# Maxima of v and of the first weight group taken across partitions on GpSimd instead of TensorE, with new durations in the planner

## The chip, the cores and the metric

One core of one Trainium2 chip. The metric is the device time of one execution in microseconds (us), as the median of several runs. The engines are named as in the profile: PE is TensorE (PEld its weight loads), DVE VectorE, ACT ScalarE, POOL GpSimd, SP SyncE, which issues the DMAs.

## The reference, cut to what matters

```
# q, k, v: 4 x 12 x 448 x 64
scores = q @ k^T / 8 - log(448)
x = sigmoid(scores) @ v                      # heads joined: 4 x 448 x 768
u = x + real(fft(fft(x, axis=1), axis=2))
un = (u - mean(u)) / sqrt(var(u) + 1e-6)     # over the 768 columns
x2 = u + relu(un @ w_ch1) @ w_ch2            # 768 -> 3072 -> 768
gate = sigmoid(causal conv of x2 over 5 rows)
out = (gate * (x2 @ w_val)) @ w_out
```

## The kernel before, in words

All large products but those of the attention run on operands that are split into two f16 parts, a high and a low one. A split needs a power of two that scales the tensor, and so the largest absolute value of all its elements. The elements lie over 128 partitions; each engine finds the maximum along a partition, and then the 128 maxima have to be joined. The kernel has two ways for that. `peak` (L405) multiplies the identity `eye` by the column of maxima on DVE (the tile `pd`), lets PE multiply it by a matrix of ones (`ones_r`), so that each partition gets all 128 numbers in PSUM, and reduces them on DVE. `peak_pool` (L421) gives the column to GpSimd's `partition_all_reduce`. From the joined maximum five to six tiny DVE operations (`pow2`, `scaled`) make the scales: for v of one batch `ve`, `vi`, `st`, `rt`; for a weight matrix `w1e`, `w1i`, `w1s` (or `w2...`).

The work has four batches of 448 rows and passes through these stages, which overlap. (1) 84 score steps: each makes a block of 8 matmul rows `ps_s<-q,k` (QK below, with the step's number), a sigmoid `sg` on ACT, and a block `ps_m<-sg,v` (SV); DVE adds and ACT copies finished sums into `acc`. (2) For each finished batch the Fourier mixing: folds `pm` on DVE and POOL, halves `ph`/`pl` scaled by `st`, two rounds of matmuls (`cd,ph`, then `cs,zh`). (3) A layer norm: a mean matmul `tt,ones` over column sums `tt`, squares `tt<-tt` on ACT, DVE and POOL, a variance matmul `ones,tt`, `rs` by a power on POOL, four diagonal tiles `tt<-eye,rs` on DVE, and a matmul `tt,ones` over them ("rstd" below) that spreads the result, from which `un` is made. (4) An MLP in 8 groups of 384 hidden columns (`w1`, `w2`). (5) The gated output. Weights arrive as int64 and are converted on ACT and DVE (`wabs`, `wf`). The first group is made during stages 1 to 3, the other seven during the MLP.

The order on the engines is fixed when the kernel is built. `Board` holds jobs (Python generators); each yields the engine and the tiles it needs next. Between two PE steps `pump` emits what by the planner's clock (`Clock.note`, a table of durations for each kind of operation) can start without delay. Every engine then runs its operations strictly in the order in which they were emitted. So a duration in the table changes no instruction by itself, but it can change which job comes next, on all engines and queues. `peak_pool` adds a rule of its own: what uses its result is emitted when the planner's PE time has passed the reduce by 4.0 us. Since every operation is issued through the recording helper `call` of `Timed`, all of them bear its line, L212.

Of the kernel before, what the change touches and what calls it, by code (L numbers as in the profile page):

```python
# [43 lines left out]
COLS = 384  # L44
# [16 lines left out]
class Clock:  # L61
# [90 lines left out]
    def note(self, e, op, a, k):  # L152
        if op == "matmul":
            out, w, x = a
            n = x.free_size()
            full = x.partition_size() > 64 or w.free_size() > 64
            passes = 1 if x.dtype != F32 else 4 if full else 1
            cost = passes * (max(n / 2384, 0.045) + 0.004)
            mode = full, out.partition_size() > 64 or not full
            if mode != self.mode:  # L160
                cost += 0.2
                self.mode = mode
            return self.put("PE", cost, (w, x), (out,), 0.12, tag="mm")
        if op == "dma_start":
            out, src = k["out"], k["in_"]
            start = max(self.at["SP"], self.ready("SP", src), self.free("SP", out))
            self.at["SP"] = start + 0.4
            size = out.partition_size() * out.free_size() * mybir.dt.size(out.dtype)
            self.dma = max(self.dma, start + 1.4) + size / 215e3
            done = self.dma + 0.6  # L170
            self.log.append(("SP", None, start, start, done))
            return self.touch("SP", (src,), (out,), done)
        k = dict(k)
        if op in ("memset", "tensor_copy", "reciprocal"):
            for nm, x in zip(("out", "in_"), a):
                k.setdefault(nm, x)
        if op == "partition_all_reduce":
            k = dict(out=a[0], in_=a[1])
        out = k["out"]
        reads = [v for nm, v in k.items() if nm not in ("out", "accum_out") and hasattr(v, "tensor")]  # L180
        ins = [k[nm] for nm in ("in0", "in1", "in_") if nm in k and hasattr(k[nm], "tensor")]
        writes = [out] + ([k["accum_out"]] if k.get("accum_out") is not None else [])
        n = max([out.free_size()] + [x.free_size() for x in ins])
        sb = all(x.space != PSUM for x in ins)
        shared = False
        if e == "ACT":
            cost = 0.16 + n * 0.00095 + (0.19 if len(writes) > 1 else 0)
        elif e == "POOL":
            cost = 1.03 if k.get("op") == ALU.pow else 0.41 if op == "partition_all_reduce" else 0.12 + n * (0.002 if out.dtype == F16 else 0.00224)
            shared = op == "tensor_tensor"  # L190
        elif op in ("tensor_tensor", "scalar_tensor_tensor"):
            cost = 0.147 + n / 960
            shared = sb
        elif op in ("tensor_scalar", "tensor_copy") and sb and len(writes) == 1:
            cost = 0.16 + n / 1920
            shared = n > 4
        else:
            cost = 0.147 + n / 960 + (0.083 if len(writes) > 1 else 0)
        return self.put(e, cost, reads, writes, shared=shared, tag=op)
# [40 lines left out]
def on(e, *aps, cost=0.6, go=None):  # L240
    return (e,) if isinstance(e, str) else e, aps, cost, go


def when(go):
    return (), (), 0, go
# [89 lines left out]
def body(tc, qd, kd, vd, w1d, w2d, cwd, wvd, wod, cdd, k12d, csd, eyed, out):  # L335
# [30 lines left out]
    def ps_m():  # L366
        board.force(closed)
        tag = min(closed(), key=lambda g: ck.next_free(("ps", g), 1))
        p = ps.tile([128, 512], F32, tag=tag, bufs=1, name="ps_m")
        taken[tag] = p  # L370
        return p

    def done_m(p):
        for tag, q in list(taken.items()):
            if q is p:
                del taken[tag]

    def banks(n):
        return lambda: sum(board.by(ck.next_free(("ps", g), 1) - 0.1) for g in closed()) >= n
# [16 lines left out]
    def col(nm):  # L396
        return keep.tile([128, 1], F32, tag=nm, bufs=4 if nm in ("st", "rt", "x2e") else 2, name=nm)
# [4 lines left out]
    def peak(m, nm):  # L402
        yield on("DVE", m, eye)
        t = col(nm + "t")
        V.tensor_reduce(out=t, in_=m, axis=AX.X, op=ALU.max)  # L405
        d = keep.tile([128, 128], F32R, tag="pd", bufs=2, name="pd")
        V.tensor_scalar(out=d, in0=eye, scalar1=t, scalar2=None, op0=ALU.mult)
        yield on("PE", d, go=banks(1))
        p = ps_m()
        T.matmul(p[:, :128], ones_r, d, start=True, stop=True)  # L410
        yield on("DVE", p[:, :128])
        g = col(nm + "g")
        V.tensor_reduce(out=g, in_=p[:, :128], axis=AX.X, op=ALU.max)
        done_m(p)
        return g

    def peak_pool(m, nm):
        yield on("DVE", m)
        t = col(nm + "t")
        V.tensor_reduce(out=t, in_=m, axis=AX.X, op=ALU.max)  # L420
        yield on("POOL", t)  # L421
        g = col(nm + "g")
        P.partition_all_reduce(g, t, 128, ABSMAX)
        then = ck.at["POOL"] + 4.0
        yield when(lambda: board.by(then))
        return g

    def pow2(g, nm, upper=False):

        e = col(nm + "e")  # L430
        if upper:
            V.tensor_scalar(out=e.bitcast(I32), in0=g.bitcast(I32), scalar1=0x07F00000, scalar2=3, op0=ALU.bitwise_and, op1=ALU.logical_shift_left)
            V.scalar_tensor_tensor(out=e.bitcast(I32), in0=g.bitcast(I32), scalar=0x40000000, in1=e.bitcast(I32), op0=ALU.bitwise_and, op1=ALU.bitwise_or)
        else:
            V.tensor_scalar(out=e.bitcast(I32), in0=g.bitcast(I32), scalar1=0x7F800000, scalar2=None, op0=ALU.bitwise_and)
        V.tensor_scalar(out=e, in0=e, scalar1=2.0 ** -90, scalar2=2.0 ** 90, op0=ALU.max, op1=ALU.min)
        i = col(nm + "i")
        V.reciprocal(out=i, in_=e)
        return e, i
# [51 lines left out]
    def split_weight(pl, scratch, src, res, shape, exp, nm, bufs=1, early=False):  # L491

        n = shape[1] * shape[2]
        t = wp.tile([128, n], F32, tag="wf", bufs=1, name="wf")
        m = keep.tile([128, 18], F32, tag="wm", bufs=2, name="wm")
        yield from to_f32(scratch, src, t, n, m, W_RANK if early else 4)
        g = yield from (peak if early else peak_pool)(m[:, :n // COLS], nm)
        yield on("DVE", g)
        e, i = pow2(g, nm, True)
        s = scaled(i, 2.0 ** exp, nm + "s")  # L500
        yield when(lambda: not isinstance(pl, Later) or pl.at is not None)
        hi = pl.tile(shape, F16, tag=nm + "hi", bufs=bufs, name=nm + "hi")
        lo = pl.tile(shape, F16, tag=nm + "lo", bufs=bufs, name=nm + "lo")
        res += [hi, lo, e]
        h, l = (x.rearrange("p a b -> p (a b)") for x in (hi, lo))
        for c in range(0, n, n // 4):
            cc = slice(c, c + n // 4)
            if early:
                yield on("ACT", t[:, cc], s, cost=0.76)
                A.activation(out=h[:, cc], in_=t[:, cc], func=AF.Copy, scale=s)  # L510
                yield on("DVE", h[:, cc])
                V.scalar_tensor_tensor(out=l[:, cc], in0=t[:, cc], scalar=s, in1=h[:, cc], op0=ALU.mult, op1=ALU.subtract)
            else:
                yield on("ACT", t[:, cc], s, cost=0.76)
                A.activation(out=t[:, cc], in_=t[:, cc], func=AF.Copy, scale=s)
                yield on("ACT", t[:, cc], cost=0.68)
                A.activation(out=h[:, cc], in_=t[:, cc], func=AF.Copy)
                yield on("POOL", h[:, cc])
                P.tensor_tensor(out=l[:, cc], in0=t[:, cc], in1=h[:, cc], op=ALU.subtract)
# [95 lines left out]
    def scale_v(b):  # L615
        m = keep.tile([128, NT], F32, tag="vm", bufs=2, name="vm")
        for j in range(NT):
            i = b * NT + j
            yield when(lambda: i in vraw)
            x = vraw[i][:, :4 - j % 2]  # L620
            yield on("DVE", x)
            amax(x, m, j)
            maxed.add(i)
        g = yield from peak(m, "v")
        yield on("DVE", g)
        e, i = pow2(g, "v")
        st = scaled(i, 2.0 ** X_EXP, "st")
        rt = scaled(e, 2.0 ** -X_EXP, "rt")
        st_of[b] = st, rt
# [520 lines left out]
    for part, n in blocks:  # L1150
        g, b = n // B, n % B
# [167 lines left out]
```

## Time and profile before

| | |
|---|---|
| median of 3 runs | 1036.89 us (1036.79 to 1037.39) |
| the profiled execution: its time, its span | 1034.22 us, 1032.4 us |
| busy: PE, DVE, ACT, POOL | 1017.3, 699.3, 427.2, 175.4 us |

The span runs from the first to the last instruction that the profiler saw in one execution; 1.8 us of that execution's time lie outside it. The rows further below are of this execution, in us from the start of its span.

### The profile page before, as it was taken

How to read it: one execution, taken by the hardware profiler on the slowest of the kernel's cores; microseconds unless marked ns; L12 is line 12 of the kernel's file. 1: busy time of each engine (PE TensorE's matmuls, PEld its weight loads, DVE VectorE, ACT ScalarE, POOL GpSimd, SP SyncE). 2: the span in 40 equal slices, each digit the busy share in tenths (PEclk: the TensorE clock that was granted, in tenths of full speed). 3: DMA queues.
4: the chain of work that ended last, by engine and by line, in shares of the span. 5: the costliest groups of instructions: out<-in, count | busy, mean ns of one | idle time of the engine just before them, and what ended most of it. 6: DMA issues, size and time to landing. Idle time of an engine off the chain costs nothing.

```text
span 1032.4 us, 15544 instructions
## 1 busy us (share of the span) xinstructions
PE 1017.3 (99%) x6116; PEld 530.8 (51%) x6116; DVE 699.3 (68%) x1486; ACT 427.2 (41%) x633; POOL 175.4 (17%) x152
## 2 busy tenths in 40 slices
PE   9999999989999999999999999999999999999998
PEld 4354455665554555555555555555555455555554
DVE  4858888988567766666776657666777876775530
ACT  6776766333332234333233331333323745333321
POOL 0104412132201212220221220222202530000000
PEclk9999999999999999999999999999999999999999
DMA  7652230011233322223322312232331000000001
GB/s 230 200 187 92 86 124 2 3 35 43 62 92 93 92 62 78 61 77 92 92 77 62 85 53 75 66 91 52 87 93 48 1 1 1 10 36 37 37 30 69
DMA packets 33033, 72.57 MB, mean 70 GB/s; under 512 B 3860, under 2 KB 15552, under 8 KB 32960
## 3 DMA queue, kind: packets, MB, share of 16 engines
q1 hardware_dynamic: 32960, 71.58, 23.9%
q8 instruction: 48, 0.79, 0.3%
q14 instruction: 25, 0.20, 0.1%
HBM read 65.88 MB, written 5.51 MB: 69 GB/s over the span
## 4 chain that ended last, share of the span: by engine, by line
PE 89%; DVE 6%; ACT 2%; POOL 1%; issue 1%; DMA 0%; ACTq 0%; SPq 0%; DVEq 0%
PE ps_m L212 56%; PE ps_s L212 33%; DVE wf L212 1%; DVE acc L212 1%; DVE gp L212 1%; DVE pm L212 1%; ACT wf L212 1%; DVE wabs L212 0%; POOL w1lo L212 0%; POOL un L212 0%; DVE tt L212 0%; DMA w<-w2d 0%; POOL w2lo L212 0%; ACT w2hi L212 0%; ACT w1hi L212 0%
## 5 line engine op out<-in xcount | busy, mean ns | idle before, releaser
L212 PE MATMUL ps_s<-un,w1hi 128*128 128x448 f16 x1152 | 312.0, 352 | 0.0
L212 PE MATMUL ps_m<-hh,w2lo 128*128 128x448 f16 x576 | 203.0, 352 | 0.5 <-POOL w2lo L212 0.5
L212 PE MATMUL ps_m<-hh,w2hi 128*128 128x448 f16 x576 | 203.0, 352 | 0.0
L212 PE MATMUL ps_s<-un,w1lo 128*128 128x448 f16 x576 | 203.0, 352 | 0.0
L212 PE MATMUL ps_m<-hl,w2hi 128*128 128x448 f16 x576 | 203.0, 352 | 0.0
L212 DVE SCALAR_TENSOR_TENSOR acc<-ps_m,rg,acc 128x448 f32<-128x448 f32 x192 | 130.8, 682 | 59.7 <-PE ps_m L212 57.6
L212 PEld LDWEIGHTS <-w2hi 128*128 128x128 f16 x1152 | 112.6, 98 | 104.6 <-issue 0.5
L212 PEld LDWEIGHTS <-w1hi 128*128 128x128 f16 x1152 | 112.3, 98 | 105.0 <-issue 1.2
L212 DVE SCALAR_TENSOR_TENSOR wf<-w,wf 128x384 int32<-128x384 int32 x240 | 135.2, 563 | 5.7
L212 DVE SCALAR_TENSOR_TENSOR hl<-ps_s,hh 128x896 f16<-128x896 f32 x64 | 54.9, 857 | 116.9 <-ACT hh L212 116.6
L212 ACT ACTIVATE wabs<-w 128x384 f32<-128x384 f32 x112 | 60.8, 554 | 165.5 <-DMA w<-w1d 48.1
L212 ACT ACTIVATE sg<-ps_s,logb 128x896 f32<-128x896 f32 x84 | 83.6, 1006 | 33.4 <-PE ps_s L212 32.5
L212 ACT ACTIVATE hh<-ps_s 128x896 f16<-128x896 f32 x64 | 46.4, 725 | 106.5 <-PE ps_s L212 106.5
L212 PE MATMUL ps_m<-sg,v 64*64 64x448 f32 x672 | 83.4, 542 | 1.1 <-DVE acc L212 1.1
L212 PEld LDWEIGHTS <-w2lo 128*128 128x128 f16 x576 | 56.4, 98 | 53.8 <-POOL w2lo L212 1.3
L212 PEld LDWEIGHTS <-w1lo 128*128 128x128 f16 x576 | 56.4, 98 | 52.6
L212 PE MATMUL ps_s<-q,k 64*64 64x448 f32 x672 | 82.7, 538 | 0.5 <-ACT sg L212 0.5
L212 DVE SCALAR_TENSOR_TENSOR gp<-acc,cw,gp 128x448 f32<-128x448 f32 x84 | 62.0, 740 | 25.7 <-ACT gp L212 23.7
L212 PE MATMUL ps_m<-xs,wvhi 128*128 128x448 f16 x288 | 78.0, 352 | 0.0
L212 DVE TENSOR_SCALAR_CACHE_REDUCE wabs<-wabs 128x384 f32<-128x384 f32 x120 | 65.4, 545 | 2.2 <-ACT wabs L212 2.1
L212 DVE TENSOR_SCALAR wf<-wabs 128x384 int32<-128x384 int32 x120 | 43.2, 360 | 13.1 <-POOL w1lo L212 7.8
L212 PE MATMUL ps_m<-xs,wvlo 128*128 128x448 f16 x144 | 50.8, 352 | 0.0
(155 smaller groups left out, 1145.0 us busy)
## 6 DMA issues: line engine op xcount, KB each, us to landing
w<-w1d SPq DMA_DIRECT2D x48, 384.0 KB
w<-w2d SPq DMA_DIRECT2D x48, 384.0 KB
q<-qd SPq DMA_DIRECT2D x24, 224.0 KB
out<-o SPq DMA_DIRECT2D x24, 224.0 KB
k<-kd SPq DMA_DIRECT2D x23, 224.0 KB
w<-wvd SPq DMA_DIRECT2D x12, 384.0 KB
w<-wod SPq DMA_DIRECT2D x12, 384.0 KB
v<-vd SPq DMA_DIRECT2D x12, 256.0 KB
```

The costliest lines, as they stand in the source:

```text
L212: return f(*a, **k)
```

## The change

Two calls of `peak` become calls of `peak_pool`: the one for v (once for each of the four batches) and the one for the first weight group (once for `w1`, once for `w2`). The four calls of `peak` for `x2` late in the kernel stay. The planner's durations change in the second and third decimal: a one-pass matmul of 448 columns counts 0.1885 instead of 0.1919 us, a float32 one 0.006 instead of 0.004 us above its columns, an ACT operation some 1% less, and operations with more than 4 columns that read a scale from a tile 0.06 us more.

```
-            cost = passes * (max(n / 2384, 0.045) + 0.004)
+            cost = passes * (max(n / 2400, 0.045) + (0.0018 if passes == 1 else 0.006))
...
+        extra = 0.06 if any(hasattr(k.get(nm), "tensor") for nm in ("scalar", "scalar1", "scale")) and n > 4 else 0.0
         if e == "ACT":
-            cost = 0.16 + n * 0.00095 + (0.19 if len(writes) > 1 else 0)
+            cost = 0.155 + n * 0.00094 + (0.19 if len(writes) > 1 else 0) + extra * (n < 600)
...
-            cost = 0.147 + n / 960
+            cost = 0.147 + n / 960 + extra
...
-            cost = 0.16 + n / 1920
+            cost = 0.16 + n / 1920 + extra
...
-        g = yield from (peak if early else peak_pool)(m[:, :n // COLS], nm)
+        g = yield from peak_pool(m[:, :n // COLS], nm)
...
-        g = yield from peak(m, "v")
+        g = yield from peak_pool(m, "v")
```

In the built program six matmuls `ps_m<-pd,ones_r` are gone from PE (5399 to 5393 matmuls), six `pd<-eye` and six reduces of PSUM from DVE, and six reduces have come to POOL. The order is another on every engine.

POOL's order before, from the first memsets of the program (row 6 there) up to the variance of batch 0; `ISA` is an instruction without a tile, `acc_96`, `acc_98`, `acc_100` and `acc_102` are `acc` of batches 0 to 3:

```order
L212 MEMSET acc_102 128x6x4
L212 ISA
L212 TENSOR_TENSOR pm<-acc_96 128x448 x3
L212 TENSOR_TENSOR pm<-acc_98 128x448 x3
L212 TENSOR_TENSOR tt<-acc_96 128x448
L212 TENSOR_TENSOR tt<-tt,acc_96 128x448
L212 TENSOR_TENSOR pm<-acc_98 128x448
L212 TENSOR_TENSOR tt<-tt,acc_96 128x448 x3
L212 TENSOR_TENSOR tt<-tt 128x448 x4
L212 TENSOR_TENSOR rs<-rs,half 112x4
L212 TENSOR_TENSOR pm<-acc_100 128x448
```

The same stretch of POOL's order now, in the changed kernel:

```order
L213 ISA
L213 TENSOR_TENSOR pm<-acc_96 128x448
L213 ISA
L213 ISA vg<-vt 128x1
L213 ISA w1g<-w1t 128x1
L213 ISA
L213 TENSOR_TENSOR pm<-acc_96 128x448 x2
L213 TENSOR_TENSOR pm<-acc_98 128x448
L213 ISA
L213 ISA vg<-vt 128x1
L213 ISA
L213 TENSOR_TENSOR pm<-acc_98 128x448 x4
```

Each visit to the reduce now stands between two bare ISA rows: v of batch 0 and `w1` share the first visit, v of batch 1 has the second.

POOL's order now at the two later visits of the early part, v of batch 2 and then v of batch 3 with `w2`; the first row is from the norm of batch 0:

```order
L213 TENSOR_TENSOR tt<-tt 128x448 x3
L213 ISA
L213 ISA vg<-vt 128x1
L213 ISA
L213 TENSOR_TENSOR rs<-rs,half 112x4
...
L213 TENSOR_TENSOR tt<-tt 128x448 x2
L213 ISA
L213 ISA vg<-vt 128x1
L213 ISA w2g<-w2t 128x1
L213 ISA
L213 TENSOR_TENSOR pm<-acc_102 128x448
L213 TENSOR_TENSOR rs<-rs,half 112x4
```

The third visit stands between the squares and the power of the norm of batch 0, the fourth between those of batch 1.

DVE's order before, from the maxima of v of batch 0 and of `w1` on:

```order
L212 TENSOR_REDUCE vt<-vm 128x1
L212 TENSOR_SCALAR pd<-eye,vt 128x128
L212 SCALAR_TENSOR_TENSOR wf<-w_316,wf 128x384 x2
L212 TENSOR_REDUCE w1t<-wm 128x1
L212 TENSOR_SCALAR pd<-eye,w1t 128x128
L212 TENSOR_REDUCE vg<-ps_m 128x1
L212 TENSOR_SCALAR ve<-vg 128x1
...
L212 TENSOR_SCALAR rt<-ve 128x1
L212 TENSOR_REDUCE w1g<-ps_m 128x1
L212 TENSOR_TENSOR acc_96<-acc_96,ps_m 128x448
```

The same place in DVE's order now:

```order
L213 TENSOR_REDUCE w1t<-wm 128x1
L213 TENSOR_TENSOR acc_96<-acc_96,ps_m 128x448
L213 TENSOR_TENSOR pm<-acc_96 128x448
L213 TENSOR_SCALAR ve<-vg 128x1
...
L213 TENSOR_SCALAR rt<-ve 128x1
L213 TENSOR_REDUCE vm<-v 128x1
L213 TENSOR_SCALAR w1e<-w1g 128x1
...
L213 TENSOR_SCALAR w1s<-w1i 128x1
L213 TENSOR_TENSOR acc_96<-acc_96,ps_m 128x448
L213 TENSOR_TENSOR pm<-acc_96 128x448
```

The sum into `acc_96` moved ahead of the scales; the scales, and behind them the next sum into `acc_96`, now stand behind a result of POOL.

## Rows read from the trace of the kernel before

**Rows 1.** The page, busy time and share of the span

```profile
PE 1017.3 (99%) x6116; PEld 530.8 (51%) x6116; DVE 699.3 (68%) x1486; ACT 427.2 (41%) x633; POOL 175.4 (17%) x152
```

**Rows 2.** Waits of PE by releaser: total us, times, longest us

```profile
PE ps_m L212 <- DVE pd L212: 4.3, 4, 1.6
```

**Rows 3.** Timeline of PE at the first two pd: start, us, operation [idle before <-releaser]

```profile
32.88 0.94 PE L212 MATMUL ps_s<-q,k 64*64 64x448 f32 x8
34.98 0.33 PE L212 MATMUL ps_m<-pd,ones_r 128*128 128x128 f32 x1 [1.16 <-DVE pd L212]
36.43 0.33 PE L212 MATMUL ps_m<-pd,ones_r 128*128 128x128 f32 x1 [1.12 <-DVE pd L212]
...
37.49 0.93 PE L212 MATMUL ps_s<-q,k 64*64 64x448 f32 x8
...
43.51 0.93 PE L212 MATMUL ps_s<-q,k 64*64 64x448 f32 x8
```

**Rows 4.** Timeline of PE: norms of batches 0 and 2, a lone pd

```profile
95.57 1.02 PE L212 MATMUL ps_m<-tt,ones 128*128 128x448 f32 x2 [0.85 <-POOL tt L212]
...
106.79 0.93 PE L212 MATMUL ps_s<-q,k 64*64 64x448 f32 x8
...
108.71 0.93 PE L212 MATMUL ps_s<-q,k 64*64 64x448 f32 x8
...
116.62 1.15 PE L212 MATMUL ps_m<-tt,ones 112*128 112x112 f32 x8
...
119.36 1.20 PE L212 MATMUL ps_m<-cd,ph 128*113 128x385 f16 x6
...
122.80 1.07 PE L212 MATMUL ps_m<-sg,v 64*64 64x448 f32 x6
...
210.95 1.15 PE L212 MATMUL ps_m<-tt,ones 112*128 112x112 f32 x8 [2.15 <-DVE tt L212]
```

**Rows 5.** Timeline of PE, the first of four pd of x2

```profile
815.94 0.33 PE L212 MATMUL ps_m<-pd,ones_r 128*128 128x128 f32 x1 [1.56 <-DVE pd L212]
```

**Rows 6.** Timeline of POOL at the first reduce that the kernel before makes there

```profile
268.52 0.41 POOL L212 PARTITION_ALL_REDUCE w1g<-w1t  x1 [15.92 <-DVE w1t L212]
276.80 4.99 POOL L212 TENSOR_TENSOR w1lo<-wf,w1hi 128x576 f16<-128x576 f32 x4 [7.87 <-ACT w1hi L212]
```

**Rows 7.** Waits of POOL by releaser: total us, times, longest us

```profile
POOL w2lo L212 <- issue: 38.1, 5, 8.0
```

**Rows 8.** Timelines of DVE and ACT behind the reduce at 268.52

```profile
269.47 0.14 DVE L212 TENSOR_SCALAR w1e<-w1g 128x1 int32<-128x1 int32 x1
...
270.42 0.78 ACT L212 ACTIVATE wf<-wf,w1s 128x576 f32<-128x576 f32 x1 [8.30 <-DVE w1s L212]
```

**Rows 9.** Timelines of POOL, DVE and ACT in the score stage

```profile
30.10 1.58 POOL L212 TENSOR_TENSOR pm<-acc 128x448 f32<-128x448 f32 x1 [29.11 <-DVE acc L212]
...
43.80 1.58 POOL L212 TENSOR_TENSOR pm<-acc 128x448 f32<-128x448 f32 x1 [4.18 <-DVE acc L212]
...
102.42 2.35 POOL L212 TENSOR_TENSOR tt<-tt 128x448 f32<-128x448 f32 x2 [1.49 <-ACT tt L212]
...
110.80 1.31 POOL L212 TENSOR_TENSOR rs<-rs,half 112x4 f32<-112x4 f32 x1 [1.83 <-DVE rs L212]
...
115.05 0.28 DVE L212 TENSOR_SCALAR tt<-eye,rs 112x112 f32<-112x112 f32 x1
...
40.97 0.78 ACT L212 ACTIVATE w1hi<-wf,w1s 128x576 f16<-128x576 f32 x1
41.65 0.99 ACT L212 ACTIVATE sg<-ps_s,logb 128x896 f32<-128x896 f32 x1
```

**Rows 10.** Timeline of PE at the start of the span

```profile
1.03 4.19 PE L212 MATMUL ps_m<-ones 128*128 128x128 f32 x18 [1.03 <-DVE logb L212]
```

**Rows 11.** Windows: length, busy PE, PEld, DVE, ACT, POOL, granted clock, DMA share, GB/s

```profile
1028.50:1032.00 3.50, 0.17 (x1) 0.00 (x0) 0.00 (x0) 0.63 (x1) 0.00 (x0) 1.00 0.17 66
1032.00:1036.00 4.00, 0.00 (x0) 0.00 (x0) 0.00 (x0) 0.00 (x0) 0.00 (x0) 0.75 0.00 0
```

## The prediction

> **What bounds the kernel now.** I read the busy times first: PE works 1017.3 of 1032.4 us [rows 1], so the whole kernel holds about 15 us in which PE stands still, and no change that leaves the matmuls alone can gain more than that. The second view is PE's waits by releaser: the largest is the tile `pd`, 4.3 us in four waits [rows 2]. That is what `peak` costs directly. The third view is PE's timeline at these places, because a wait is only part of the price (the matmul and the change of tile shape come on top). In the score stage PE alternates QK and SV blocks; eight of them take 43.51 - 37.49 = 6.02, so 0.7525 us each [rows 3]. From QK19 at 32.88 to QK20 at 37.49 are two blocks, 1.51 us, and the two pd of v and `w1`; these cost 4.61 - 1.51 = **3.1 us** [rows 3]. A pd whose maxima are there in time costs 108.71 - 106.79 - 1.51 = **0.4 us** [rows 4]; two more in the score stage are like it. The fourth reading is PE's later waits: 2.15 us on `tt` before the rstd matmul of batch 2 [rows 4], and 1.56 us on the first pd of x2 [rows 5].
>
> **What a visit to the reduce costs.** The later groups show it, where GpSimd has time. The reduce takes 0.41 us at 268.52, but POOL's next operation starts at 276.80, 7.87 us after its end [rows 6]. That this is no wait for data shows in POOL's waits: before `w2lo` it stood five times for 38.1 us in all, 7.6 each, and waited for nothing that the profile shows [rows 7]. The bare ISA row behind each reduce in the order sits exactly there: something is loaded back. I take **7.7 us** behind each visit. The result itself is out early: DVE starts `w1e` at 269.47, 0.95 us after the reduce's start, and ACT uses `w1s` 0.95 later, at 270.42 [rows 8].
>
> Ahead of each reduce stands the same ISA row, but its time can't be read: POOL was idle for 15.92 us there until DVE had the column [rows 6], so a load could hide in it. Its bounds are 0 and 15.9. I take 7.7 too, by the nearest row, the same instruction behind the reduce. The planner counts 0.41 us for the whole visit, so it places other POOL work around it as if POOL were free.
>
> The Trainium skill (GPSIMD Engine Reference, 2.1 Instruction dispatch) says that the first call to freshly loaded GpSimd code pays a load of about 6 us that no instruction in the profile shows; the gaps here are longer, 7.6 to 7.9 [rows 6, 7]. With its 6 us ahead of each reduce the sum below would be about +3 instead of +10.
>
> **The change part by part.** Four visits come into the early part. Times are those of before, until the place in question.
>
> A, v of batch 0 and `w1`. POOL ends its first fold at 30.10 + 1.58 = 31.68 [rows 9]. With the load, `vg` runs to 31.7 + 7.7 + 0.4 = 39.8 and `w1g` from there; ACT can use `w1s` 0.95 + 0.95 later, at 41.7. In ACT's order `w1hi` stands ahead of the sigmoid of QK22, as before; it takes 0.7 (40.97 to 41.65), the sigmoid 1.0 [rows 9], so QK24, which needs the bank that this sigmoid frees, starts at about 43.8. Before it started at 43.51, with the 3.1 us of both pd in it [rows 3]. So the pd are gone and the wait for the sigmoid takes their place: +0.3. POOL's other two folds come after the load back, at 40.2 + 7.7 = 47.9 and later; the last of them began at 43.80 before [rows 9]. It is some 5 us late, the halves `ph` are late after it, and ACT's in-order queue holds a sigmoid behind `ph`: an estimate of +0.4 (0 to 1). A together **+0.7**. If the load were nothing, A would be -3.1, and it stays there up to a load of 4 us, since the column of `w1` is ready only shortly before its pd at 36.43 [rows 3].
>
> B, v of batch 1. POOL has only folds around it, which have slack; the lone pd goes: **-0.2** (-0.4 to 0).
>
> C, v of batch 2, is the dear one, since it stands between the squares and the power of batch 0's norm. The mean matmul is at 95.57 [rows 4]; POOL's third square ends at 102.42 + 2.35 = 104.77 [rows 9], 9.2 behind it. Then load 7.7, reduce 0.4, load back 7.7, power 1.3 [rows 9], four diagonals of 0.28 [rows 9]: 27.4 behind the mean. PE's rstd matmul has its place 116.62 - 95.57 = 21.0 behind the mean, less 0.4 for the pd that stood between, 20.6 [rows 4]; the order now has as many blocks there. So PE waits 27.4 - 20.6 = 6.8; less the pd itself, 0.4: **+6.4** (without the first load -0.4).
>
> D, v of batch 3 with `w2`, the same in batch 1's norm, with two squares on POOL instead of three: they end some 8.3 behind the mean (estimate: 9.2 less most of a square). Then 7.7 + 0.4 + 0.4 + 7.7, a fold 1.4 that stands ahead of the power, power 1.3, diagonals 1.1: 28.3. PE's place for rstd is there 20 blocks (15.1 us), two Fourier steps of 122.80 - 119.36 = 3.4 [rows 4] and about 1 us each for mean and variance matmul behind the mean's start: 23.9. So 4.4 late, first part of it at the variance matmul, since the scales of v on DVE hold squares behind them; and a sum into `acc` that is queued on DVE behind the diagonals keeps a PSUM bank from PE for some 1.5 more. Removed: a pd, 0.4, and the wait of 2.15 on `tt` at 210.95, since batch 2's norm now falls elsewhere. **+3.3**.
>
> x2. Its four pd stay, but the order has ten matmuls instead of five between the maxima and the first pd, so of the 1.56 us [rows 5] about 1.0 goes: **-1.0**.
>
> The clock. The first nine matmuls of 128 columns take 4.19 us [rows 10], where one of 448 columns in the score stage takes 1.02 [rows 4], so the nine would take some 2.2 there: PE begins at the lower of its two levels, 1.2 GHz, and loses 2.0 us. At the end, with PE idle from 1028.7 on (0.17 us busy in the window from 1028.5), the granted clock of the window from 1032 on has fallen to 0.75 on the mean [rows 11]. Whether it falls in the wait at C too, and costs 2.0 afterwards, is open: **+1.0** (0 to 2).
>
> The planner's durations, otherwise: a reshuffle with no visible place of its own; 0 (-1.5 to +1.5, as the waits of about 1 us of before would go or come). DVE loses six diagonals and six reduces of 0.28 us, but does not bound.
>
> Sum: 0.7 - 0.2 + 6.4 + 3.3 - 1.0 + 1.0 = **+10.2 us**. On the profiled execution this is 1034.2 to 1044.4; its time lies 2.7 below the median of the runs shown, and the difference applied to the median gives 1036.9 + 10.2 = **1047**.
>
> **The rivals.** (1) The load ahead of the reduce is short or is done ahead of time. For it: no row shows it. Against it: the same instruction behind the reduce shows 7.7. With nothing there, A is -3.1, B -0.4, C -0.4 (the diagonals come at 19.7, before PE's place at 20.6), D -2.5, x2 -1.0: -7.4, so **about 1030**, faster. It decides at a load of about 5 us: at 5, A -2.1, C +3.7, D +0.2 to -0.9, B and x2 -1.2, sum about 0. Below that every us saves about 1 at C and at first at D; above it A, C and D each pay.
> (2) A load ahead of about 6 us: A -1.0, B -0.2, C +4.7, D +0.7, x2 -1.0, the clock perhaps +0.3: **about 1040**, slower all the same. The rule of the skill's page above would end here.
> (3) The load ahead takes most of the 15.9 us bound: A, C and D each pay 7 us more, **about 1070**.
> (4) PE's clock falls at C and again at D, or DVE's order behind `ve<-vg` starves PE of banks for longer than I count: **1050 to 1054**.
> (5) The planner's durations do more than the visits, to either side; bounded above by the 15 us of idle time, but no place for it is seen.
>
> **How the numbers follow.** My forecast, a load of 6.5 to 9 ahead and 7.7 behind: 0.50 (1042 to 1051). Rival 2 or a load a little shorter than it: 0.18, of which 0.07 lands within 0.2%. Rival 1: 0.17, nearly all of it faster. Rival 3: 0.03, rival 4: 0.07, rival 5: 0.05, split between the signs. A measurement of this kernel can tell about 0.2%, 2.1 us. Together: faster 0.20, the same 0.08, slower 0.72. The range that leaves out 2 in 10 runs from the edge of rival 1 to rival 4: 1031 to 1054; the slower cases alone lie in 1039 to 1054.
>
> **What would show it right or wrong.** In POOL's timeline each early reduce should have about 7.7 us behind it with nothing shown, and the first reduce of visit A should end near 39.8 although its column was ready by about 35: this reads off the load ahead directly. PE should show one wait of 6 to 7 us ahead of the rstd matmul of batch 0, waits of together 5 to 6 us around the norm of batch 1, no wait on the pd of v, and in the windows behind C a granted clock that tells whether it fell. The prediction is wrong if `vg` starts at once when its column is there, if POOL's power in C comes less than 9 us behind its last square, or if PE's new waits stand elsewhere than at the norms.

## The result, and the profile after

The changed kernel takes 1049.58 us (median of 4 runs, 1048.34 to 1050.71) against 1036.84 for the kernel before (the three runs of its table and a fourth): a ratio of 1.0134, with a 95% interval from 1.0114 to 1.0154, so 12 to 16 us more. The profiled execution took 1048.71 us, 14.5 more than that of before.

The page of the changed kernel, busy times, and below it PE's waits by releaser (columns as in [rows 2]):

```profile
PE 1021.5 (98%) x6110; PEld 537.3 (51%) x6110; DVE 705.0 (67%) x1478; ACT 425.6 (41%) x626; POOL 177.6 (17%) x161
```
```profile
PE ps_m L213 <- DVE zl L213: 6.5, 2, 4.0
PE ps_m L213 <- DVE tt L213: 5.8, 3, 5.2
PE ps_s L213 <- ACT sg L213: 4.3, 2, 3.9
PE ps_m L213 <- DVE e L213: 3.3, 1, 3.3
```

The waits on `pd` of [rows 2], 4.3 us, are gone, those for x2 [rows 5] too. In their place stand 20 us of others, the four rows above. And PE is 4.2 us longer busy [rows 1] with six matmuls fewer: part of its work ran at a lower clock.

The timeline of POOL in the changed kernel, the four visits and what follows each (the rows of [rows 6] and [rows 9] answer to these), and below it from DVE's timeline the rows that make the column of the first and of the third visit:

```profile
29.91 1.59 POOL L213 TENSOR_TENSOR pm<-acc 128x448 f32<-128x448 f32 x1 [28.93 <-DVE acc L213]
39.87 0.41 POOL L213 PARTITION_ALL_REDUCE vg<-vt  x1 [8.37 <-issue]
40.20 0.43 POOL L213 PARTITION_ALL_REDUCE w1g<-w1t  x1
47.71 2.49 POOL L213 TENSOR_TENSOR pm<-acc 128x448 f32<-128x448 f32 x2 [7.09 <-DVE vm L213]
...
75.49 0.41 POOL L213 PARTITION_ALL_REDUCE vg<-vt  x1 [6.75 <-DVE w1lo L213]
83.10 2.26 POOL L213 TENSOR_TENSOR pm<-acc 128x448 f32<-128x448 f32 x2 [7.21 <-issue]
...
102.81 2.36 POOL L213 TENSOR_TENSOR tt<-tt 128x448 f32<-128x448 f32 x2 [1.89 <-ACT tt L213]
111.14 0.41 POOL L213 PARTITION_ALL_REDUCE vg<-vt  x1 [5.97 <-DVE rs L213]
120.61 1.05 POOL L213 TENSOR_TENSOR rs<-rs,half 112x4 f32<-112x4 f32 x1 [9.05 <-issue]
...
170.46 1.14 POOL L213 TENSOR_TENSOR tt<-tt 128x448 f32<-128x448 f32 x1 [2.55 <-DVE tt L213]
177.39 0.41 POOL L213 PARTITION_ALL_REDUCE vg<-vt  x1 [5.79 <-issue]
177.72 0.43 POOL L213 PARTITION_ALL_REDUCE w2g<-w2t  x1
185.21 1.12 POOL L213 TENSOR_TENSOR pm<-acc 128x448 f32<-128x448 f32 x1 [7.06 <-DVE rs L213]
```
```profile
34.26 0.16 DVE L213 TENSOR_REDUCE vt<-vm 128x1 f32<-128x6 f32 x1
...
107.12 0.16 DVE L213 TENSOR_REDUCE vt<-vm 128x1 f32<-128x6 f32 x1
```

Now the load ahead of a visit can be read: 8.37 us at the first, where the column came after 3 us of it and could not be the reason; 5.97 and 5.79 at the third and fourth. At the third the column came after 2.1 us of it, at the fourth it was there before, and the length is nearly the same: the load does not wait for the column. The way back costs 7.1 to 7.2 us, and 9.05 where the power comes next. Of the load ahead the Trainium skill (GPSIMD Engine Reference, 2.1 Instruction dispatch) says about 6 us; the third and fourth visit agree, the first is longer.

The timeline of PE, all waits over 0.4 us between 40 and 250 us, with the blocks behind the first, the small waits at the two rstd matmuls (124.03 and 187.82) and the mean matmul of batch 1 (163.50):

```profile
44.28 1.08 PE L213 MATMUL ps_s<-q,k 64*64 64x448 f32 x8 [3.89 <-ACT sg L213]
45.08 1.37 PE L213 MATMUL ps_m<-sg,v 64*64 64x448 f32 x8
46.01 1.93 PE L213 MATMUL ps_s<-q,k 64*64 64x448 f32 x8
...
122.03 1.67 PE L213 MATMUL ps_m<-tt,ones 112*128 112x112 f32 x6 [5.21 <-DVE tt L213]
124.03 0.77 PE L213 MATMUL ps_m<-tt,ones 112*128 112x112 f32 x2 [0.33 <-DVE tt L213]
...
144.64 2.29 PE L213 MATMUL ps_m<-sg,v 64*64 64x448 f32 x8 [4.04 <-DVE zl L213]
...
163.50 1.02 PE L213 MATMUL ps_m<-tt,ones 128*128 128x448 f32 x2
...
187.82 1.12 PE L213 MATMUL ps_m<-tt,ones 112*128 112x112 f32 x8 [0.28 <-DVE tt L213]
...
192.27 0.91 PE L213 MATMUL ps_m<-sg,v 64*64 64x448 f32 x2 [2.44 <-DVE zl L213]
...
231.36 0.37 PE L213 MATMUL ps_m<-k,e 76*113 76x385 f16 x1 [3.34 <-DVE e L213]
```

The waits at 44 and 122 are where the prediction put them. At the norm of batch 1 (187.82) hardly any is left. Those at 144.64, 192.27 and 231.36 were not foreseen. The windows behind the waits (columns as in [rows 11]):

```profile
44.30:48.00 3.70, 3.70 (x28) 2.36 (x32) 3.20 (x6) 2.58 (x4) 0.29 (x1) 0.68 0.03 6
...
122.00:126.00 4.00, 3.65 (x16) 2.46 (x20) 4.00 (x7) 0.00 (x0) 2.18 (x2) 0.50 0.00 0
144.60:147.00 2.40, 2.36 (x14) 1.54 (x18) 2.40 (x5) 0.00 (x0) 0.00 (x0) 0.51 0.88 324
192.30:196.00 3.70, 3.70 (x24) 1.47 (x26) 3.26 (x4) 0.83 (x2) 3.17 (x2) 0.54 0.02 4
...
231.30:234.00 2.70, 2.64 (x16) 2.14 (x17) 1.68 (x3) 1.16 (x3) 1.76 (x1) 1.00 0.00 0
```

Behind four of the five waits the granted clock is at its lower level, 1.2 GHz (0.50), for all or part of the window. Length times the missing share gives 1.2, 2.0, 1.2 and 1.7 us for these windows, an estimate of 6.1 in all; behind some of them the clock stays low a little longer.

### The profile page after: what moved, and what is told of

Same layout as the page of the kernel before. It is cut to its first block, busy times and chain, and to the rows that moved or that the text cites. A ratio compares the mean times of both kernels' runs of the same rounds, so it can differ in the third digit from the quotient of the medians.

```text
span 1046.9 us, 15521 instructions
## 1 busy us (share of the span) xinstructions
PE 1021.5 (98%) x6110; PEld 537.3 (51%) x6110; DVE 705.0 (67%) x1478; ACT 425.6 (41%) x626; POOL 177.6 (17%) x161
## 4 chain that ended last, share of the span: by engine, by line
PE 91%; DVE 3%; issue 3%; ACT 1%; POOL 1%; POOLq 0%; ACTq 0%; DVEq 0%
PE ps_m L213 56%; PE ps_s L213 34%; DVE pm L213 1%; DVE tt L213 1%; ACT sg L213 0%; DVE wf L213 0%; POOL w1lo L213 0%; ACT wf L213 0%; ACT w1hi L213 0%; DVE e L213 0%; DVE acc L213 0%; POOL rs L213 0%; DVE wabs L213 0%; POOL un L213 0%; DVE w2lo L213 0%
## 5 line engine op out<-in xcount | busy, mean ns | idle before, releaser
L213 ACT ACTIVATE wabs<-w 128x384 f32<-128x384 f32 x105 | 57.6, 555 | 150.0 <-DVE wf L213 54.2
L213 PE MATMUL ps_m<-sg,v 64*64 64x448 f32 x672 | 87.0, 563 | 6.5 <-DVE zl L213 6.5
L213 PE MATMUL ps_s<-q,k 64*64 64x448 f32 x672 | 85.1, 555 | 4.3 <-ACT sg L213 4.3
L213 PEld LDWEIGHTS ps_s<-q,k 64*64 64x64 f32 x672 | 30.4, 137 | 40.5 <-issue 25.2
```

The costliest lines, as they stand in the source:

```text
L213: return f(*a, **k)
```

## The experiments

Two theories at the start. **L**: the loads around the visits cost the time. **O**: the new order costs it, whatever GpSimd does. The table has all thirteen kernels; each ratio is to the kernel before, in runs on the same chip, so it can differ a little from what the medians alone give.

| kernel | median us | ratio, 95% interval |
|---|---|---|
| the change | 1049.58 | 1.0134, 1.0114 to 1.0154 |
| its order, no early loads | 1036.20 | 1.0005, 0.9990 to 1.0020 |
| planner's durations alone | 1034.51 | 1.0000, 0.9984 to 1.0016 |
| the visits, old durations | 1054.39 | 1.0183, 1.0154 to 1.0211 |
| that order, no early loads | 1031.33 | 0.9953, 0.9939 to 0.9967 |
| planner told of the loads | 1052.24 | 1.0162, 1.0135 to 1.0189 |
| no load in visit A | 1047.78 | 1.0108, 1.0089 to 1.0127 |
| no load in visit C | 1041.17 | 1.0050, 1.0031 to 1.0068 |
| no load in visit D | 1050.07 | 1.0128, 1.0106 to 1.0150 |
| before, pd's matmul later | 1036.48 | 1.0001, 0.9989 to 1.0014 |
| no early loads, sums behind zl | 1035.49 | 1.0001, 0.9989 to 1.0013 |
| new durations, sums behind zl | 1039.61 | 1.0039, 1.0022 to 1.0056 |
| before, sums behind zl | 1035.58 | 1.0006, 0.9991 to 1.0021 |

**The changed order without the loads.** Only the reduce itself is exchanged, and the planner is told nothing of it:

```
-        P.partition_all_reduce(g, t, 128, ABSMAX)
+        if nm == "v" or early:
+            ck.note("POOL", "partition_all_reduce", (g, t, 128, ABSMAX), {})
+            nc.gpsimd.tensor_tensor(out=g, in0=t, in1=t, op=ALU.add)
+        else:
+            P.partition_all_reduce(g, t, 128, ABSMAX)
```

> The changed kernel with every instruction in its place on every engine; only the six early reduces on GpSimd are replaced by a plain addition of the column to itself, so that no maximum is joined across partitions there (the scales of v and of the first weight group are then each partition's own). What is taken away is the load ahead of and behind each of the four visits. Theory L (the loads cost the time): GpSimd's chain in the norm of batch 0 ends 13 us earlier, PE's waits of 3.9 us at 44 and of 5.5 us ahead of the first rstd matmul go, those on zl at 144.6 (4.0) and 192.3 (2.4) go too, since DVE runs late only because of the first ones, and the lowered clock behind them: 1032 to 1037 us. Theory O (the new order costs the time, whatever GpSimd does): the waits on zl and the wait of 3.3 us on e at 231 stay, with their clock: 1041 us or more.

1036.2 us, 13 below the change. So the loads cost 13 us, as L has it. What went can be counted in the traces: the rows of POOL's sequencer have 90 records named MODIFY_POOL_CONFIG in the changed kernel and 74 here, four fewer for each of the four visits. None of them lasts over 0.083 us; the time lies in the gaps beside them. But the timeline of PE in this kernel, two of its waits:

```profile
131.66 2.29 PE L213 MATMUL ps_m<-sg,v 64*64 64x448 f32 x8 [4.04 <-DVE zl L213]
...
216.56 0.57 PE L213 MATMUL ps_m<-k,e 76*113 76x385 f16 x1 [3.34 <-DVE e L213]
```

They are as long as with the loads, to 0.01 us. So they belong to the order, as O has it. L's reason for the first (DVE late through the loads) falls. The third of the kind, 2.44 us on `zl` at 192.27, belongs in part to the loads: without them it is 1.81.

**The durations alone, and the visits alone.** One kernel takes the change without its last two hunks, the other only these two.

> The kernel before with the changed durations of the planner alone; all six early maxima stay with peak. Theory L: within 4 us of before, 1033 to 1040 us, since no GpSimd load is added. Theory O: the new durations by themselves bring new waits of PE in the norms and the Fourier steps: 1042 us or more.

> The kernel before with the two calls of peak_pool, and the old durations in the planner. Theory L: slower than before by 8 to 16 us, 1045 to 1053 us, with a PE wait of 4 us or more at the first visit (about 44 us) and one of 5 us or more ahead of the rstd matmul of batch 0. Theory O: within 4 us of before, since the old durations keep the order that suits the chip.

The durations alone change nothing (1.0000). The visits under the old durations are the slowest kernel of all, 1.4 us above the range that L gave. Where they wait, in PE's timeline of that kernel, and below it POOL's at visit C:

```profile
44.21 1.87 PE L212 MATMUL ps_s<-q,k 64*64 64x448 f32 x8 [3.42 <-ACT sg L212]
...
121.68 1.65 PE L212 MATMUL ps_m<-ones,tt 128*112 128x1 f32 x8 [9.83 <-POOL tt L212]
...
205.85 0.38 PE L212 MATMUL ps_m<-cs,zl 112*6 112x256 f32 x1 [4.33 <-DVE zl L212]
```
```profile
113.34 0.41 POOL L212 PARTITION_ALL_REDUCE vg<-vt  x1 [5.94 <-issue]
120.51 1.12 POOL L212 TENSOR_TENSOR tt<-tt 128x448 f32<-128x448 f32 x1 [6.76 <-issue]
```

In that order visit C stands ahead of the last square instead of behind it, so the variance matmul waits for both loads, 9.8 us. And v of batch 3 and `w2` do not share a visit there: their reduces are 18 us apart, at 175.64 and 193.66, so it has five pairs of loads (94 of the records named above). O is wrong about this pair: the old durations do not help.

> The two new calls with the planner's old durations, every instruction where that kernel has it, but the six early reduces replaced by an addition of the column to itself (the scales are each partition's own): no load. Theory L (the loads, not the order): 1054.4 us fall by about as much as the changed kernel did without its loads (13 us) or more, since here the third visit cost 9.8 us of waiting at the variance matmul: 1034 to 1041 us. If the order with the old durations is bad in itself: 1043 us or more.

With the same exchange as above the old order gives 1031.3 us, below the range expected, 23 below its own kernel with loads and 0.5% below the kernel before. So the loads' price depends on the order: 13 us in one, 23 in the other. The 0.5% is what the removal of the six `pd` brings in this order, and no such kernel exists here that also joins the maxima.

**The visits one by one.** The exchange in one visit only, all else in place.

> The changed kernel with every instruction in its place; only in the first visit to the reduce (v of batch 0 and w1) the reduces are replaced by an addition of the column to itself, so that these two scales are each partition's own, and the visit's two loads are gone. Theory S (the visits' prices add up, each the wait read in the trace and the clock behind it): PE's 3.9 us wait on the sigmoid near 44 shrinks to below 1, and the blocks at the lower clock behind it (1.7 us) go: 1049.6 - 5 = 1044 us (1043 to 1046). Theory M (the time is made up elsewhere: what is saved here is waited for at the next norm): 1047 us or more.

> The same for the third visit alone (v of batch 2, between the squares and the power of batch 0's norm). Theory S: the 5.5 us wait ahead of the rstd matmul goes, and with it about 2.4 us at the lower clock: 1049.6 - 8 = 1042 us (1040 to 1044). The 4.0 us wait on zl near 144 stays, as it did with no load at all. Theory M: 1046 us or more, with a longer wait on zl.

> The same for the fourth visit alone (v of batch 3 and w2, in batch 1's norm). Theory S by the trace of the changed kernel: only the 0.3 us ahead of the rstd matmul and 0.6 us of the wait on zl behind it hang on the visit, so 1048 to 1050 us. By the sum of the prediction it would be worth 5.8 us: 1044 us.

C is worth 0.84% or 8.7 us, and in its kernel PE has no wait over 0.4 us between 60 and 130. A is worth 2.7 us and D 0.6; with intervals of 0.2% on both sides neither stands clear of zero by itself. Theory S expected 5 for A: PE's wait there did fall, from 3.9 to 0.2 and 0.8, but its four runs lie between 1045.2 and 1049.2, and the traced one is the lowest. The three sum to 12.0 of the 13.4; the second visit was not tried by itself, and the rest of 1.4 is within the noise. As far as these intervals tell, what the visits cost adds up. The clock blurs it: the wait on `e` is 3.34 or 3.35 us in each of these kernels, but in the 3 us behind it the granted clock is 1.00 in the changed kernel and in A's, and 0.50 in C's and D's. By length times the missing share that is 1.5 us in these windows alone, an estimate.

**A planner that knows.** The planner counts 6.0 us ahead of a visit and 7.2 behind it.

```
+        if pooled:
+            self.at["POOL"] += -7.2 if self.lib else 6.0
...
+            if pooled:
+                self.at["POOL"] += 7.2
...
-        then = ck.at["POOL"] + 4.0
+        then = ck.at["POOL"] - 3.2
```

The last line keeps the rule of 4.0 us behind the reduce, now that 7.2 are added to POOL's time.

> The changed kernel, with a planner that counts 6.0 us ahead of a visit to the reduce and 7.2 us behind it as busy time of GpSimd. Theory L: the loads are still there, but the norm's power, diagonals and rstd matmul are placed later, so PE finds other work: most of the 5.5 us wait of batch 0 and the clock behind it go; the first visit's wait on the sigmoid can't go, since w1's scale is late in any order, unless its operation is placed behind the sigmoids: 1036 to 1044 us. Theory O: another reshuffle, no clear gain: 1045 to 1052 us.

L's number was missed: 1052.2 us. PE's timeline in this kernel, three of its waits, and rows of DVE's timeline ahead of the last:

```profile
53.04 0.98 PE L221 MATMUL ps_s<-q,k 64*64 64x448 f32 x8 [0.38 <-ACT sg L221]
117.23 1.11 PE L221 MATMUL ps_m<-tt,ones 112*128 112x112 f32 x8 [0.39 <-DVE tt L221]
...
220.48 0.57 PE L221 MATMUL ps_m<-k,e 76*113 76x385 f16 x1 [9.62 <-DVE e L221]
```
```profile
211.49 0.37 DVE L221 TENSOR_TENSOR eo<-r 12x223 f32<-12x223 f32 x1
211.79 1.83 DVE L221 COPY eo<-r 12x2 f32<-12x2 f32 x1
...
215.61 0.15 DVE L221 COPY eo<-r 12x2 f32<-12x2 f32 x1
```

The planner did hide the loads: at the first visits and ahead of the first rstd matmul PE waits 0.4 us each. But it splits both visits that had shared their loads (six pairs of loads, 98 of the records), and the chain `eo`, `e` (the special rows of the last batch's Fourier step) came so late on DVE that PE waited 9.6 us for it; a further 4.9 us went to a `pd` of x2. Why the planner put that chain there was not traced.

**Can the waits be had otherwise?** First `peak` with its matmul emitted 1.5 us later:

```
+        then = ck.at["DVE"] + 1.5
+        yield when(lambda: board.by(then))
         yield on("PE", d, go=banks(1))
```

> The kernel before, with peak as it was and the old durations, but the matmul over pd is emitted only when the planner's PE time has passed the making of pd by 1.5 us, so that other blocks stand between. If the waits of 4.3 us on pd are what can be had here: 1.5 to 4 us faster than before. If a new order costs as much as it saves, as the planner's durations alone did: within 2 us of before.

Same time as before. The waits on `pd` are down to 0.2 us, but a wait of 3.74 us on a sum into `acc` has come at 126.77. Then the waits on `zl`: a condition ahead of the six symmetric sums `pm<-pm`, which in the changed order stand ahead of the four `zl` on DVE.

```
+            yield when(lambda: b == 0 or b - 1 in rounded)
             for k in range(2):
...
             yield when(lambda: zs.count(0) + zs.count(1) == 4)
+            rounded.add(b)
```

> The changed kernel without the six early loads, and with one condition more: the symmetric sums on DVE over the folds of a batch (the six pm operations) are emitted only when the batch before has its four zl. If the 4.0 and 1.8 us waits on zl are what ate the gain of the removed pd: they go, with the lowered clock behind the first, and the time is 4 to 7 us below that kernel without the condition: 1029 to 1033 us. If other lateness takes their place: 1035 us or more.

> The planner's new durations with peak for all six early maxima, as before, and the same condition on the six pm operations. Its two waits on zl (1.4 and 3.0 us) and the lower clock behind them should go: 3 to 5 us below before, 1031 to 1033 us. If other lateness takes their place: 1035 us or more.

> The kernel before with that condition alone. It had no wait on zl above 0.4 us, so within 2 us of before; where the condition delays the halves of a batch so that PE waits on them, slower.

None gains; with the new durations and `peak` it costs 0.4%: there both waits on `zl` stay (1.42 and 2.95 us), and one of 2.0 on `tt` is new. In the first of the three the wait of 1.8 us on `zl` and that of 3.3 on `e` did go, but as much came elsewhere: 2.0 on `tt`, 1.4 on `w2lo` and 1.1 on `w1hi`. The longest, 4.01 us on `zl` at 131.56, stayed. DVE's timeline ahead of it:

```profile
127.72 1.80 DVE L213 TENSOR_SCALAR wf<-wabs 128x384 int32<-128x384 int32 x1
129.55 1.15 DVE L213 SCALAR_TENSOR_TENSOR wf<-w,wf 128x384 int32<-128x384 int32 x2
130.62 0.35 DVE L213 TENSOR_SCALAR wabs<-w 128x384 int32<-128x384 int32 x1
130.88 2.19 DVE L213 SCALAR_TENSOR_TENSOR zl<-ps_m,rt,zh 113x385 fp32r<-113x385 f32 x4
```

The conversion of weights moved into the place of the sums, and the four `zl` start at 130.88 where they started at 130.99. So taking the sums from in front of `zl` does not bring `zl` forward, because other work is emitted in their place. That the place where the planner emits `zl` is the cause fits this, but no run moved `zl` itself.

## Why the prediction came out as it did

The forecast was +10.2 us and 1047, the measurement +12.7 and 1049.6. The sign was right, the size near, and the cause that it named, the loads on both sides of the visits, is shown: without them the time is that of before. That the sum came so near is partly luck. By the forecast the loads are worth 17.6 us, from -7.4 without any (rival 1) to +10.2; the ratios with and without them, 1.0134 and 1.0005, are 13.4 us apart. Without loads the forecast had -7.4 and the runs +0.5. An error of 4 us to one side met one of 8 to the other. Visit by visit, clock included, the loads were worth 3.8 at A, 7.8 at C and 5.8 at D by the forecast, and 2.7, 8.7 and 0.6 in the runs.

Of the signs that were named beforehand, the gaps in POOL's timeline and the wait ahead of batch 0's rstd matmul came; of the 5 to 6 us around the norm of batch 1 only 0.28 did. One sign of being wrong came too: of the 19.9 us of new waits 9.8 stand on `zl` and `e` of the Fourier steps, not at the norms and not at visit A.

- **The visit's price.** Load and load back at 7.7 us each. Measured: at A 8.4 ahead and 7.1 behind, at C 6.0 and 9.05, at D 5.8 and 7.1. That a load stands on both sides of a reduce was the decisive step and is shown; taking the size ahead from the row behind was too long by 1.7 to 1.9 at C and D, too short by 0.7 at A. Rivals 1 and 3, no load or one of 15.9 us, fall. Rival 2 had the right length for C and D but, at about 1040, too small a sum.
- **A, +0.7.** The wait on the sigmoid is there (3.89 us, for the 3.1 of both `pd`). The clock behind it was not counted.
- **C, +6.4 and +1.0 for the clock.** PE waited 5.5 us (5.21 and 0.33) where 6.8 were worked out, and then ran at half clock. Without the load the kernel is 8.7 us faster. The place and the chain were right, though the two loads came out at 15.0 for 15.4 only because one was shorter and the other longer than taken. The clock's term was half of what it became: 0.50 over the 4 us from 122, so 2.0 in that window. For the nine matmuls at the start, from which the 2.0 was taken, the trace shows a granted clock of 1.00 (1.03 to 5.22), so their slowness is not shown to be the clock.
- **D, +3.3.** This term failed. PE's rstd matmul started 187.82 - 163.50 = 24.3 us behind the mean, close to the 23.9 forecast as its place. It could, since the diagonals came almost in time, 4.0 us before the 28.3 worked out: the two loads were together 2.5 shorter than twice 7.7, fold and power 0.5, the squares ended 0.2 earlier, and PE could begin 0.4 behind the start of the diagonals instead of behind all four. Without these loads the kernel is only 0.6 us faster.
- **"The planner's durations, otherwise: 0."** This failed too, the other way. The prediction let the gains stand (the 2.15 us wait, the `pd`), which gave -7.4 without a load. With the old durations that is nearly what was measured, -4.9 (1031.3; rival 1 said 1030). With the new ones nothing was left of it (1036.2): in the trace of that kernel PE waits 9.2 us on `zl` and `e`, where under the old durations it waits 0.3, and behind two of these waits the granted clock falls (0.57 from 131.6 to 138, 0.50 from 216.5 to 222; length times the missing share, an estimate, is 5.5 us). Alone, on `peak`, the same durations cost nothing: they bring waits on `zl` there too (1.42 and 2.96 us), but others go, such as the 2.15 on `tt`. So the two halves of the change do not add up, and the text had looked at each by itself. Which choice of the planner does it was not traced.
- **x2, -1.0.** The two waits on its `pd` are gone (2.05 us), twice what was counted.

## What to carry to other kernels

Cost a call like GpSimd's `partition_all_reduce` by the gaps around it, not by its busy time: here 0.4 us of work had gaps of about 6 us ahead and 7 us behind, and the place in the queue decides whether anyone waits. When an instruction order comes from a planner, a change of its table and a change of its jobs are not two terms of a sum; build the same order without the suspected cost (same places, cheaper instruction) and time it, since this separates the cost from the reshuffle. Three experiments here that took one wait away found others in its place, so read the trace of the miss before the next edit.

## What the runs showed of the hardware that was not expected

The load ahead of the first visit to the reduce was longer than later ones: 7.43 to 8.37 us in the five kernels whose first visit is at about 40 us, against 5.8 to 6.5 later, where nothing else was waited for. The power as first instruction behind a reduce came 6.87 to 9.40 us after it in five places (9.05 in the changed kernel), where a fold in the changed kernel came after 7.1 to 7.2.

Some small DVE operations took much longer beside work of POOL. In the kernel whose planner knows, a copy of 12x2 took 1.83 us beside POOL's `un` (211.63 to 215.44 us) and 0.15 otherwise. In the changed kernel `e` took 2.39 at 228.91, beside POOL's `un` from 228.94 on, for 0.68 at the three other places; the difference of 1.71 is about half of PE's 3.34 us wait there. That POOL is the cause was not tested.

The length of a wait did not tell whether PE's granted clock fell. In the changed kernel it fell in a wait of 2.44 us (0.54 behind it) and not in one of 3.34 us (1.00 behind it). The same wait of 3.34 us, at the same place of the same order, was followed by 0.50 in the kernel without early loads. What tells these apart was not tried.
